# Fifth term of the first product for two of eight hidden units: from four full matmuls to pairs of 64-row matmuls beside the convolution, with a new order of all steps

## The chip, the cores and the metric

The kernel runs on one core of one Trainium2 chip. The metric is the device time of one execution in microseconds (us), the median of several runs. The engines are TensorE (PE; its weight loads are listed apart, as PEld), VectorE (DVE), ScalarE (ACT), GpSimd (POOL), and SyncE (SP), which here only issues transfers.

## The reference, cut to what matters

A causal convolution of 7 taps over 4096 tokens (8 batches, 192 channels, one softmaxed kernel per head of 24 channels) feeds a two-layer network whose activation is a rational function:

```python
out = np.einsum('hk,bskhg->bshg', softmax(weight), x_unf)      # convolution
x = out.reshape(32768, 192)
h = x @ w_in                                                   # 192 -> 2048, first product
P = a[0] + a[1] * h + a[2] * h2 + a[3] * h3
Q = 1.0 + np.abs(b[0]) * np.abs(h) + np.abs(b[1]) * h2
return ((P / (Q + 1e-06)) @ w_out).astype(np.float32)          # 2048 -> 192, second product
```

## The kernel before, in words

The 32768 tokens are 64 chunks of 512. The 2048 hidden features are eight units of 256, and each unit is two halves (j = 0, 1) of 128 features. So a chunk has: one convolution (step c), eight units of the first product (g1, two pieces a and b each), eight rational functions (steps hs, p, u, v, A, B, Q, L, Y, m, e, g, each on a tile of 128 x 1024), eight units of the second product (g2, four pieces each) and two stores (O).

The first product keeps more than one pass of precision by splitting both operands: x = xh + xl and w = wh + wl, each part rounded to the fp32r format. The 192 channels are 128 (part 0) and 64 (part 1). For part 0 three products are summed: wh xh, wl xh, wh xl. For part 1 the tile xB holds xh of the 64 channels in rows 0 to 63 and xl of the same channels in rows 64 to 127, and the weights of part 1 are stored twice, in rows 0 to 63 and again in rows 64 to 127; so wh on xB gives wh xh + wh xl in one matmul, and wl on xB gives wl xh (and the negligible wl xl) in another. That is five matmuls of 128 rows x 512 columns for each half of a unit (L362 to L369), ten for a unit, eighty for a chunk. The fifth is wl on xB.

The convolution (L304 to L313) is 72 small matmuls on tiles of 64 rows x 32 columns, two row halves by four column groups of the array, each of 58 tokens; being plain fp32, each becomes two instructions of the profile, 144 for a chunk. Its result goes to two PSUM banks (o0, o1), which the second product of the chunk before has just left; ACT copies it out rounded (xh), DVE takes the rest (xl), and small SBUF-to-SBUF transfers on SP's queue (move, gaps) put the parts in their places.

The order of the steps is written out by hand in three texts: START (chunks 0 to 2 and the preparation of the weights), PLAN (one period, repeated for chunks 3 to 62), END. A step "g16a.2" is piece a of unit 6 of the first product, of the chunk two before the period's own. Each engine executes its steps in the order of the text; semaphores hold back a step whose data or buffer isn't there. In a period PE does: the convolution of chunk i, units 6 and 7 of the first product of chunk i-2, then units 0 to 5 of chunk i-1, and between these the second product of chunk i-2. The PSUM tile of a unit (hp, ps_h) has two buffers, so a unit's first matmul waits for the last reader of the unit two before it: hs, A and B on ACT, v on DVE. The tile y (ps_y, PSUM) has one buffer: Y of a unit on ACT waits for g of the unit before on DVE, and m of a unit on DVE waits for its Y.

```python
        terms = ((wh_t, 0, xhA), (wl_t, 0, xhA), (wh_t, 0, xlA), (wh_t, 1, xB), (wl_t, 1, xB))
        for n, (w, part, x) in enumerate(terms):
            nc.tensor.matmul(H[k][:, j, :], lhsT=w[:, i, part, j, :], rhs=x, start=(n == 0), stop=(n == len(terms) - 1))
```

Of the kernel before, what the change touches and what calls it, by code (L numbers as in the profile page):

```python
# [54 lines left out]


START = """
tp1.0 tp3.0 tp2.0 tp5.0 tp4.0 tp6.0 tp8.0 tp9.0 cf0.0 cf1.0 wia0.0 wis0.0 wio0.0 cf2.0 c0.0 xh0.0 wid0.0
xl0.0 xh1.0 wia1.0 xl1.0 wis1.0 wio1.0 tp0.0 wid1.0 wir0.0 wih0.0 wil0.0 g10a.0 wir1.0 wia2.0 wis2.0
wow0.0 wiw3.0 wio2.0 wid2.0 wow1.0 wod0.0 wih1.0 woa0.0 wos0.0 woo0.0 wid3.0 wir2.0 wih2.0 wia3.0 wis3.0  # L60
wor0.0 wiw4.0 g10b.0 wio3.0 wod1.0 hs0.0 B0.0 wow2.0 woa1.0 p0.0 u0.0 wip1.0 A0.0 Q0.0 wir3.0 wid4.0
wil1.0 wos1.0 woo1.0 wia4.0 g11a.0 g11b.0 hs1.0 p1.0 tp7.0 B1.0 wor1.0 wip2.0 wis4.0 wio4.0 woa2.0
wil2.0 u1.0 A1.0 Q1.0 wos2.0 woo2.0 v0.0 wih3.0 wip3.0 wiw5.0 wia5.0 wod2.0 L0.0 wow3.0 wis5.0 wor2.0
wil3.0 wiw6.0 wid5.0 Y0.0 wio5.0 woa3.0 wow4.0 g12a.0 wir4.0 g12b.0 v1.0 hs2.0 p2.0 wos3.0 m0.0 B2.0
g13a.0 g13b.0 woo3.0 u2.0 wih4.0 wip4.0 wia6.0 wod3.0 L1.0 wor3.0 wiw7.0 A2.0 e0.0 wis6.0 g0.0 hs3.0
wio6.0 woa4.0 Q2.0 wir5.0 Y1.0 v2.0 wos4.0 p3.0 wid6.0 wir6.0 wil4.0 wih5.0 wip5.0 woo4.0 wia7.0 wow5.0
wod4.0 m1.0 u3.0 g14a.0 g14b.0 wis7.0 wid7.0 e1.0 A3.0 B3.0 wio7.0 wir7.0 wih6.0 woa5.0 hs4.0 wil5.0
v3.0 wow6.0 Q3.0 wip6.0 wow7.0 wos5.0 wil6.0 wih7.0 L2.0 g1.0 B4.0 g15a.0 woo5.0 wip7.0 g15b.0 wil7.0
c0.1 Y2.0 m2.0 A4.0 hs5.0 p4.0 xh0.1 xh1.1 u4.0 v4.0 g16a.0 Q4.0 p5.0 u5.0 xl0.1 xl1.1 e2.0 B5.0 woa6.0
A5.0 wos6.0 woo6.0 woa7.0 g2.0 wos7.0 g16b.0 woo7.0 L3.0 c0.2 Q5.0 hs6.0 v5.0 g17a.0 Y3.0 g17b.0 A6.0  # L70
xh0.2 xh1.2 m3.0 xl0.2 e3.0 g3.0 g20a.0 g20c.0 B6.0 hs7.0 p6.0 u6.0 v6.0 g21a.0 g21c.0 g22a.0 L4.0
g10a.1 g10b.1 xl1.2 g20b.0 Q6.0 p7.0 g20d.0 Y4.0 g21b.0 u7.0 m4.0 B7.0 g21d.0 g22b.0 wor4.0 A7.0 Q7.0
L5.0 L6.0 e4.0 hs0.1 g4.0 Y5.0 wod5.0 v7.0 g11a.1 p0.1 m5.0 e5.0 u0.1 wod6.0 B0.1 A0.1 g11b.1 Q0.1 hs1.1
p1.1 A1.1 g5.0 Y6.0 v0.1 m6.0 e6.0 g22c.0 g23a.0 L7.0 u1.1 g22d.0 g23b.0 wor6.0 g6.0 g23d.0 B1.1 g12a.1
v1.1 g12b.1 A2.1 Q1.1 hs2.1 Y7.0 g23c.0 g24a.0 g24b.0 g24d.0 m7.0 e7.0 L0.1 g7.0 g24c.0 g13a.1 g13b.1
wor5.0 B2.1 p2.1 wod7.0 u2.1 hs3.1 A3.1 wor7.0 g25a.0 g25c.0 g26a.0 g25b.0 g26c.0 Y0.1 v2.1 m0.1 e0.1
g0.1 g14a.1 g14b.1 g25d.0 B3.1 L1.1 hs4.1 Y1.1 Q2.1 g26b.0 g26d.0 g27a.0 B4.1 g27b.0 g27d.0 g27c.0 p3.1
u3.1 A4.1 v3.1 g15a.1 L2.1 O0.0 O1.0 m1.1 e1.1 Q3.1 p4.1 g15b.1 u4.1 g1.1 Y2.1 v4.1 Q4.1 hs5.1
"""


END = """
c0.1 xh0.1 g16a.3 g16b.3 xh1.1 m2.3 xl0.1 xl1.1 L3.3 g20a.3 g20b.3 g20d.3 g21b.3 g21d.3 g20c.3 p5.3 e2.3
A5.3 u5.3 B5.3 Q5.3 hs6.3 g2.3 v5.3 Y3.3 g17a.3 L4.3 p6.3 g17b.3 u6.3 A6.3 g21a.3 g21c.3 B6.3 Q6.3 hs7.3
p7.3 m3.3 e3.3 g3.3 g22a.3 u7.3 Y4.3 g22c.3 v6.3 g10a.2 B7.3 g10b.2 L5.3 A7.3 Q7.3 hs0.2 p0.2 u0.2 m4.3
e4.3 g4.3 g22b.3 g22d.3 g23a.3 Y5.3 A0.2 v7.3 g11a.2 L6.3 B0.2 g11b.2 g23b.3 g23d.3 g24b.3 hs1.2 p1.2
m5.3 e5.3 g5.3 v0.2 Q0.2 g23c.3 Y6.3 A1.2 g12a.2 m6.3 g12b.2 u1.2 B1.2 Q1.2 g24d.3 e6.3 g6.3 L7.3 v1.2
g24a.3 hs2.2 p2.2 g25b.3 g25d.3 Y7.3 m7.3 g13a.2 g13b.2 g24c.3 g25a.3 g25c.3 g26a.3 e7.3 g7.3 B2.2 A2.2
u2.2 v2.2 g14a.2 L0.2 Q2.2 hs3.2 Y0.2 m0.2 p3.2 L1.2 A3.2 g14b.2 g26b.3 e0.2 g26c.3 g27a.3 g0.2 B3.2
u3.2 v3.2 Q3.2 hs4.2 Y1.2 m1.2 e1.2 g1.2 L2.2 A4.2 g27c.3 O0.3 g15a.2 g15b.2 g20a.2 p4.2 u4.2 B4.2  # L90
g26d.3 g27b.3 hs5.2 Y2.2 g27d.3 v4.2 g16a.2 g16b.2 B5.2 Q4.2 O1.3 m2.2 e2.2 p5.2 u5.2 g2.2 A5.2 Q5.2
v5.2 g20c.2 g21a.2 L3.2 g20b.2 g20d.2 hs6.2 p6.2 u6.2 Y3.2 m3.2 e3.2 g3.2 L4.2 g17a.2 g17b.2 B6.2 A6.2
Q6.2 v6.2 g21b.2 g21d.2 hs7.2 Y4.2 m4.2 g21c.2 L5.2 e4.2 g4.2 p7.2 u7.2 A7.2 B7.2 v7.2 Q7.2 g10a.1
g10b.1 hs0.1 p0.1 u0.1 Y5.2 L6.2 g22a.2 g22c.2 g23a.2 g23c.2 A0.1 g11a.1 m5.2 e5.2 g11b.1 B0.1 hs1.1
g22b.2 p1.1 g5.2 g22d.2 g23b.2 Y6.2 g23d.2 A1.1 v0.1 L7.2 g12a.1 B1.1 g12b.1 hs2.1 m6.2 e6.2 g6.2 Q0.1
Y7.2 B2.1 L0.1 g24b.2 g24d.2 g25b.2 u1.1 v1.1 Q1.1 g13a.1 g13b.1 m7.2 e7.2 p2.1 u2.1 g24a.2 A2.1 g24c.2
g7.2 v2.1 g14a.1 hs3.1 p3.1 g14b.1 Y0.1 m0.1 e0.1 B3.1 Q2.1 L1.1 g25d.2 g26b.2 g0.1 A3.1 g25a.2 u3.1
hs4.1 v3.1 g15a.1 Q3.1 Y1.1 B4.1 g15b.1 m1.1 e1.1 g1.1 L2.1 A4.1 p4.1 u4.1 v4.1 hs5.1 g25c.2 g26a.2 Y2.1
m2.1 e2.1 g2.1 Q4.1 g26c.2 g27a.2 p5.1 u5.1 A5.1 B5.1 v5.1 g27c.2 Q5.1 g26d.2 g16a.1 L3.1 Y3.1 m3.1 e3.1
g27b.2 g16b.1 g17a.1 g27d.2 hs6.1 O0.2 g20a.1 p6.1 g17b.1 A6.1 O1.2 g20b.1 g20d.1 g20c.1 g21a.1 g21b.1  # L100
L4.1 g3.1 Y4.1 m4.1 g21d.1 hs7.1 e4.1 g4.1 B6.1 B7.1 g21c.1 g22a.1 L5.1 Y5.1 g22b.1 u6.1 v6.1 g22c.1
g23a.1 g22d.1 g23b.1 Q6.1 g23d.1 g24b.1 p7.1 u7.1 m5.1 e5.1 g5.1 A7.1 L6.1 v7.1 Y6.1 Q7.1 g24d.1 g25b.1
m6.1 e6.1 g6.1 L7.1 Y7.1 m7.1 e7.1 g23c.1 g24a.1 g24c.1 g7.1 g25a.1 g25c.1 g26a.1 g26c.1 g25d.1 g26b.1
g26d.1 g27a.1 g27c.1 O0.1 g27b.1 g27d.1 O1.1
"""


# [1 line left out]
def kernel(  # L109
# [251 lines left out]

    def gemm1(k, j):  # L362
        c, i = divmod(k, UPC)
        xhA, xlA, xB = X[c, "A"], X[c, "L"], X[c, "B"]
        if j == 0:
            H[k] = ps_h.tile([P, 2, CH], F32, name="hp")
        terms = ((wh_t, 0, xhA), (wl_t, 0, xhA), (wh_t, 0, xlA), (wh_t, 1, xB), (wl_t, 1, xB))
        for n, (w, part, x) in enumerate(terms):
            nc.tensor.matmul(H[k][:, j, :], lhsT=w[:, i, part, j, :], rhs=x, start=(n == 0), stop=(n == len(terms) - 1))  # L369

# [190 lines left out]
```

## Time and profile before

| | us |
|---|---|
| median of 3 runs | 2677.01 (2675.8 to 2678.11) |
| profiled execution | 2675.36 |
| its span, first to last instruction | 2673.7 |
| PE busy (matmuls) | 2636.4 (99%) |
| DVE busy | 2583.7 (97%) |
| ACT busy | 2563.2 (96%) |
| POOL busy | 2313.4 (87%) |

The profiled execution took 1.7 us more than its span. Busy time is the union of an engine's instructions; instructions of one engine overlap (the next begins while the last results of the one before are being written), so the distance from start to start is shorter than the duration. Matmul ends are modelled: starts are what is to be read on PE. The chain of waits that ended last runs over PE for 92% of the span.

### The profile page before, as it was taken

The page shows a single profiled execution, that of the slowest core. Times are in us where ns is not written, and L with a number is a line of the kernel's source. Part 1 is how long each engine was busy: PE and PEld are TensorE (multiplying, and loading weights), DVE is VectorE, ACT ScalarE, POOL GpSimd, SP SyncE. Part 2 cuts the span into 40 slices and gives each one's busy share as a digit, 9 for nine tenths or more (in the row PEclk, how much of TensorE's full clock was granted, in tenths as well). Part 3 has the DMA queues.
Part 4 walks back from the last instruction along what each step waited for, and adds up shares of the span by engine and source line. Part 5 has one row for each costly group of instructions (what it writes and reads, how often), then busy time and mean ns, then how long its engine had stood idle before and what let it go on. Part 6 is the DMA issues. An engine that isn't in the chain of part 4 may idle for free.

```text
span 2673.7 us, 56816 instructions
## 1 busy us (share of the span) xinstructions
PE 2636.4 (99%) x22513; PEld 2392.6 (89%) x22513; DVE 2583.7 (97%) x2235; ACT 2563.2 (96%) x2863; POOL 2313.4 (87%) x1565
## 2 busy tenths in 40 slices
...
GB/s 198 118 137 127 131 139 125 134 136 125 137 130 130 137 124 131 139 126 132 137 127 137 126 132 136 124 135 135 129 131 134 131 137 123 131 138 124 130 125 93
DMA packets 138706, 352.25 MB, mean 132 GB/s; under 512 B 19416, under 2 KB 54488, under 8 KB 138440
## 3 DMA queue, kind: packets, MB, share of 16 engines
...
## 4 chain that ended last, share of the span: by engine, by line
PE 92%; DVE 2%; ACT 2%; issue 2%; POOL 1%; DMA 1%; ACTq 0%; POOLq 0%; DVEq 0%
PE o L387 47%; PE hp L369 42%; PE o L312 3%; DVE t L421 1%; DVE y L444 1%; POOL t L417 1%; ACT y L436 0%; ACT hs L410 0%; ACT B L433 0%; DVE t L448 0%; ACT A L424 0%; POOL t L413 0%; ACT B L427 0%; DMA A<-B 0%; PE y L321 0%
## 5 line engine op out<-in xcount | busy, mean ns | idle before, releaser
L387 PE MATMUL o<-wo_t,t 128*128 128x192 f32 x8192 | 1404.2, 326 | 1.3 <-DVE t L448 1.3
L387 PEld LDWEIGHTS o<-wo_t,t 128*128 128x128 f32 x8192 | 1354.2, 190 | 37.2 <-DVE t L448 1.9
L417 POOL TENSOR_TENSOR t<-t,hs 128x1024 f32<-128x1024 f32 x512 | 1264.1, 2469 | 32.2
L369 PE MATMUL hp<-xh,wh_t 128*128 128x512 f32 x2048 | 868.5, 424 | 9.3 <-DVE t L421 5.5
L413 POOL TENSOR_SCALAR t<-hs,cf 128x1024 f32<-128x1024 f32 x512 | 665.0, 1299 | 195.7 <-ACT hs L410 190.9
L369 PE MATMUL hp<-xh,wl_t 128*128 128x512 f32 x2048 | 803.1, 392 | 2.6 <-DVE wl_t L299 1.9
L440 DVE SCALAR_TENSOR_TENSOR t<-t,cf,y 128x1024 f32<-128x1024 f32 x512 | 655.7, 1281 | 34.3 <-ACT y L436 25.4
L421 DVE SCALAR_TENSOR_TENSOR t<-t,cf,hp 128x1024 f32<-128x1024 f32 x512 | 652.4, 1274 | 4.4 <-ACT y L436 2.3
L448 DVE SCALAR_TENSOR_TENSOR t<-y,t 128x1024 f32<-128x1024 f32 x512 | 626.8, 1224 | 17.4
L444 DVE SCALAR_TENSOR_TENSOR y<-A,y 128x1024 f32<-128x1024 f32 x512 | 625.6, 1222 | 0.0
L410 ACT COPY hs<-hp 128x1024 f32<-128x1024 f32 x512 | 519.5, 1015 | 61.9 <-PE hp L369 23.2
L430 POOL DMA_DIRECT2D A<-B x512 | 468.4, 915 | 102.8 <-ACT B L427 69.1
L436 ACT ACTIVATE y<-B 128x1024 f32<-128x1024 f32 x512 | 531.3, 1038 | 20.0 <-DVE t L448 18.5
L433 ACT ACTIVATE B<-A 128x1024 f32<-128x1024 f32 x512 | 545.2, 1065 | 4.0 <-DMA A<-B 3.9
L424 ACT ACTIVATE A<-hp 128x1024 f32<-128x1024 f32 x512 | 528.0, 1031 | 0.8 <-PE hp L369 0.8
L427 ACT ACTIVATE B<-hp 128x1024 f32<-128x1024 f32 x512 | 528.4, 1032 | 0.0
L369 PEld LDWEIGHTS hp<-xh,wh_t 128*128 128x128 f32 x2048 | 387.1, 189 | 84.0 <-DVE t L421 6.7
L369 PEld LDWEIGHTS hp<-xh,wl_t 128*128 128x128 f32 x2048 | 387.1, 189 | 66.0 <-DVE wl_t L299 2.4
L369 PE MATMUL hp<-xl,wh_t 128*128 128x512 f32 x1024 | 401.7, 392 | 0.0
L369 PEld LDWEIGHTS hp<-xl,wh_t 128*128 128x128 f32 x1024 | 193.2, 189 | 42.6 <-issue 0.4
L312 PEld LDWEIGHTS o<-wb_t,xs 64*32 64x32 f32 x9072 | 92.7, 105 | 29.3 <-issue 27.1
L312 PE MATMUL o<-wb_t,xs 64*32 64x58 f32 (+1 forms) x9072 | 102.0, 221 | 6.9 <-issue 3.9
...
## 6 DMA issues: line engine op xcount, KB each, us to landing
A<-B POOLq DMA_DIRECT2D x512, 512.0 KB, 4.8
...
out<-ob SPq DMA_DIRECT2D x128, 192.0 KB
...
xh<-xl SPq DMA_DIRECT2D x126, 48.0 KB
...
```

Of the source, the lines that this page charges most:

```text
L369: nc.tensor.matmul(H[k][:, j, :], lhsT=w[:, i, part, j, :], rhs=x, start=(n == 0), stop=(n == len(terms) - 1))
L387: nc.tensor.matmul(op[:, t, 0:D], lhsT=g[:, j * CH + tok:j * CH + tok + P], rhs=wo_t[:, f, :], start=(f == 0 and t == 0), stop=(f == FT - ...
L413: nc.gpsimd.tensor_scalar(tile_of(k, "t", tpool), st[k]["hs"], a3, a2, ALU.mult, ALU.add)
L417: nc.gpsimd.tensor_tensor(out=t, in0=t, in1=st[k]["hs"], op=ALU.mult)
L421: nc.vector.scalar_tensor_tensor(out=t, in0=t, scalar=a1, in1=flat(k), op0=ALU.add, op1=ALU.mult)
L424: nc.scalar.activation(out=tile_of(k, "A", work), in_=flat(k), func=AF.Abs, scale=scales[0])
L427: nc.scalar.activation(out=tile_of(k, "B", work), in_=flat(k), func=AF.Square, scale=scales[1])
L433: nc.scalar.activation(out=st[k]["B"], in_=st[k]["A"], func=AF.Ln, bias=C_Q)
L436: nc.scalar.activation(out=tile_of(k, "y", ps_y), in_=st[k]["B"], func=AF.Exp, scale=-1.0)
L440: nc.vector.scalar_tensor_tensor(out=t, in0=t, scalar=a0, in1=st[k]["y"], op0=ALU.add, op1=ALU.mult)
L444: nc.vector.scalar_tensor_tensor(out=y, in0=st[k]["A"], scalar=C_Q, in1=y, op0=ALU.add, op1=ALU.mult)
L448: nc.vector.scalar_tensor_tensor(out=t, in0=st[k]["y"], scalar=2.0, in1=t, op0=ALU.subtract, op1=ALU.mult)
```

## The change

For units 5 and 6 the fifth term leaves the row of five. A step h does it for both halves of the unit: half 0 as a matmul of rows 0 to 63 (weights wl rows 0 to 63, xB rows 0 to 63), half 1 as a matmul of rows 64 to 127, with the weights' second copy and a new tile xu that holds a copy of xB's rows 0 to 63 in its rows 64 to 127. The two use different halves of the array and different PSUM banks. The negligible product wl xl is left out for these units. Which matmul starts and which ends an accumulation is counted (terms_done), since h6 stands ahead of g16a and g16b and h5 behind g15b. In the repeated period PE's order becomes g15a, g15b, h5 (end of a period), c0, h6, g16a, g16b (start of the next). The copy to xu is one more transfer of 64 rows x 2 KB for each chunk on SP's queue, behind those of xl1, into a pool of two buffers. The orders of all engines are written anew.

```diff
+HALF_UNITS = (5, 6)
 PLAN = """
-c0.0 xh0.0 xh1.0 g16a.2 g16b.2 m2.2 L3.2 xl0.0 xl1.0 B5.2 A5.2 g20b.2 e2.2 g2.2 p5.2 u5.2 g20a.2 hs6.2
-Y3.2 g20c.2 g21a.2 g21c.2 v5.2 Q5.2 p6.2 A6.2 u6.2 g20d.2 m3.2 g17a.2 g17b.2 e3.2 g22a.2 L4.2 g3.2 B6.2
...
-g25d.2 g0.1 g26b.2 g26d.2 hs4.1 g27b.2 g27d.2 Y1.1 L2.1 p4.1 O0.2 A4.1 O1.2 u4.1 v3.1 m1.1 e1.1 g1.1
-B4.1 g15a.1 g15b.1 Y2.1 v4.1 hs5.1 Q4.1
+c0.0 Y2.2 hs5.2 m2.2 A5.2 xh0.0 xh1.0 e2.2 B5.2 Q4.2 xl0.0 h6.2 xl1.0 g2.2 g16a.2 g16b.2 L3.2 hs6.2 p5.2
+u5.2 g20a.2 g20c.2 v5.2 Y3.2 g20b.2 m3.2 g20d.2 Q5.2 L4.2 g21a.2 e3.2 g17a.2 g17b.2 A6.2 p6.2 g21c.2
...
+g14b.1 hs4.1 Q3.1 g0.1 Y1.1 L2.1 g25b.2 g25d.2 g26b.2 g26d.2 g27c.2 v3.1 m1.1 B4.1 g27b.2 A4.1 g27d.2
+g15a.1 g15b.1 e1.1 p4.1 O0.2 h5.1 O1.2 u4.1 g1.1 v4.1
 """
 START = """
...
+u3.0 wil6.0 B3.0 wih7.0 wip7.0 A3.0 Q3.0 v3.0 g15a.0 L2.0 hs4.0 p4.0 woo5.0 wow7.0 wil7.0 Y2.0 m2.0
+A4.0 e2.0 c0.1 B4.0 xh0.1 xh1.1 xl0.1 g15b.0 h5.0 hs5.0 xl1.1 u4.0 v4.0 woa6.0 wos6.0 wor4.0 woo6.0 h6.0
+g16a.0 g2.0 g16b.0 L3.0 B5.0 woa7.0 wos7.0 woo7.0 A5.0 p5.0 u5.0 v5.0 c0.2 g17a.0 Q4.0 Q5.0 hs6.0 p6.0
...
+    zpool = ctx.enter_context(tc.tile_pool(name="zpool", bufs=2))
...
             gaps(xB[BLK:], xl, 104, 2)
+            upper_copy(c)
+
+    def upper_copy(c):
+        X[c, "U"] = zpool.tile([P, CH], F32R, name="xu")
+        move(X[c, "U"][BLK:], X[c, "B"][0:BLK])
...
+    terms_done = {}
+
+    def term(k, j, w, x, **kw):
+        if k not in H:
+            H[k] = ps_h.tile([P, 2, CH], F32, name="hp")
+        n = terms_done[k, j] = terms_done.get((k, j), 0) + 1
+        nc.tensor.matmul(H[k][:, j, :], lhsT=w, rhs=x, start=(n == 1), stop=(n == 5), **kw)
 
     def gemm1(k, j):
...
+        for w, part, x in ((wh_t, 0, xhA), (wl_t, 0, xhA), (wh_t, 0, xlA), (wh_t, 1, xB)):
+            term(k, j, w[:, i, part, j, :], x)
+        if i not in HALF_UNITS:
+            term(k, j, wl_t[:, i, 1, j, :], xB)
+
+    def gemm1_halves(k):
+        c, i = divmod(k, UPC)
+        for j, x in enumerate((X[c, "B"], X[c, "U"])):
+            rows = slice(BLK * j, BLK * j + BLK)
+            term(k, j, wl_t[rows, i, 1, j, :], x[rows], tile_position=(BLK * j, 0))
```

## Rows read from the trace of the kernel before

**Rows 1.** The page: busy time, share of the span and instructions of each engine.

```profile
PE 2636.4 (99%) x22513; PEld 2392.6 (89%) x22513; DVE 2583.7 (97%) x2235; ACT 2563.2 (96%) x2863; POOL 2313.4 (87%) x1565
```

**Rows 2.** Windows: stretch, length, busy of PE to POOL, granted clock, DMA.

```profile
0.00:106.30 106.30, 79.86 (x685) 63.58 (x685) 83.58 (x108) 85.17 (x116) 77.80 (x68) 0.89 0.67 164
...
1004.98:1045.77 40.79, 40.79 (x353) 37.20 (x353) 40.04 (x35) 39.63 (x45) 35.83 (x25) 1.00 0.64 132
...
2560.30:2673.70 113.40, 106.16 (x583) 95.94 (x570) 103.03 (x87) 97.61 (x107) 85.14 (x57) 1.00 0.53 106
...
147.08:2560.30 2413.22, 2409.60 (x20913) 2195.89 (x20912) 2357.61 (x2008) 2341.20 (x2598) 2115.30 (x1417) 1.00 0.64 131
```

**Rows 3.** Waits from 147.08 to 2560.30: waiter, releaser, us in total, times, longest.

```profile
PEld o L312 <- issue: 21.1, 58, 0.8
...
DVE t L440 <- ACT y L436: 16.8, 68, 0.6
...
PE hp L369 <- DVE t L421: 1.8, 3, 0.8
```

**Rows 4.** Timeline of PE around one convolution: start, us, instruction.

```profile
1004.67 0.39 PE L369 MATMUL hp<-xh,wl_t 128*128 128x512 f32 x1
1004.98 1.59 PE L312 MATMUL o<-wb_t,xs 64*32 64x58 f32 x144
1006.51 0.50 PE L369 MATMUL hp<-xh,wh_t 128*128 128x512 f32 x1
1006.84 0.39 PE L369 MATMUL hp<-xh,wl_t 128*128 128x512 f32 x1
1007.07 0.39 PE L369 MATMUL hp<-xl,wh_t 128*128 128x512 f32 x1
...
1008.92 4.06 PE L387 MATMUL o<-wo_t,t 128*128 128x192 f32 x24
```

**Rows 5.** Timeline of PE's weight loads around the same convolution.

```profile
1004.44 0.19 PEld L369 LDWEIGHTS hp<-xh,wl_t 128*128 128x128 f32 x1
1004.98 1.46 PEld L312 LDWEIGHTS o<-wb_t,xs 64*32 64x32 f32 x144 [0.35 <-issue]
1006.50 0.19 PEld L369 LDWEIGHTS hp<-xh,wh_t 128*128 128x128 f32 x1
1006.61 0.19 PEld L369 LDWEIGHTS hp<-xh,wl_t 128*128 128x128 f32 x1
```

**Rows 6.** Groups by shape: the convolution's matmuls, busy us, mean ns, idle before.

```profile
L312 PE MATMUL o<-wb_t,xs 64*32 64x58 f32 x8064 | 91.7, 221 | 3.0 <-DVE wo_t L284 3.0
```

**Rows 7.** Timeline of DVE from 1041 to 1053, over one start of a period.

```profile
1041.73 1.28 DVE L440 SCALAR_TENSOR_TENSOR t<-t,cf,y 128x1024 f32<-128x1024 f32 x1
...
1045.36 1.28 DVE L421 SCALAR_TENSOR_TENSOR t<-t,cf,hp 128x1024 f32<-128x1024 f32 x1
1046.57 1.28 DVE L440 SCALAR_TENSOR_TENSOR t<-t,cf,y 128x1024 f32<-128x1024 f32 x1
1048.00 1.29 DVE L339 TENSOR_TENSOR xl<-o,xh 128x512 fp32r<-128x512 f32 x2 [0.15 <-ACT xh L330]
...
1053.11 1.28 DVE L440 SCALAR_TENSOR_TENSOR t<-t,cf,y 128x1024 f32<-128x1024 f32 x1 [0.24 <-ACT y L436]
```

**Rows 8.** Timeline of ACT over the same start of a period.

```profile
1045.51 1.03 ACT L436 ACTIVATE y<-B 128x1024 f32<-128x1024 f32 x1 [0.24 <-DVE t L448]
1046.47 1.01 ACT L410 COPY hs<-hp 128x1024 f32<-128x1024 f32 x1
...
1052.01 1.07 ACT L436 ACTIVATE y<-B 128x1024 f32<-128x1024 f32 x1
```

**Rows 9.** Timeline of PE in START, around the convolution of chunk 2.

```profile
61.73 1.82 PE L312 MATMUL o<-wb_t,xs 64*32 64x58 f32 x128 [2.99 <-DVE wo_t L284]
66.00 0.41 PE L312 MATMUL o<-wb_t,xs 64*32 64x48 f32 x14 [2.46 <-issue]
```

**Rows 10.** The page: transfers by issuing queue: count, KB each.

```profile
xh<-xl SPq DMA_DIRECT2D x126, 48.0 KB
```

More of the change, by code (lines that the diff above doesn't have):

```diff
@@ L44 @@
 PLAN = """
-c0.0 xh0.0 xh1.0 g16a.2 g16b.2 m2.2 L3.2 xl0.0 xl1.0 B5.2 A5.2 g20b.2 e2.2 g2.2 p5.2 u5.2 g20a.2 hs6.2
-Y3.2 g20c.2 g21a.2 g21c.2 v5.2 Q5.2 p6.2 A6.2 u6.2 g20d.2 m3.2 g17a.2 g17b.2 e3.2 g22a.2 L4.2 g3.2 B6.2
-hs7.2 v6.2 g21b.2 Y4.2 g21d.2 g22b.2 L5.2 m4.2 Q6.2 e4.2 B7.2 A7.2 g10a.1 g10b.1 g4.2 p7.2 g22d.2 g23b.2
-g23d.2 g24b.2 hs0.1 u7.2 p0.1 Y5.2 A0.1 v7.2 L6.2 B0.1 m5.2 e5.2 Q7.2 g11a.1 g11b.1 hs1.1 g22c.2 g5.2
-u0.1 g23a.2 g23c.2 g24a.2 Y6.2 p1.1 Q0.1 v0.1 g12a.1 g12b.1 g24d.2 B1.1 A1.1 L7.2 m6.2 e6.2 g6.2 hs2.1
@@ L50 @@
-g25b.2 u1.1 Q1.1 p2.1 Y7.2 v1.1 B2.1 m7.2 u2.1 e7.2 g24c.2 g25a.2 A2.1 g13a.1 g13b.1 L0.1 g7.2 hs3.1
-Q2.1 Y0.1 p3.1 g25c.2 g26a.2 v2.1 g26c.2 g27a.2 m0.1 L1.1 A3.1 g14a.1 g14b.1 B3.1 u3.1 Q3.1 e0.1 g27c.2
-g25d.2 g0.1 g26b.2 g26d.2 hs4.1 g27b.2 g27d.2 Y1.1 L2.1 p4.1 O0.2 A4.1 O1.2 u4.1 v3.1 m1.1 e1.1 g1.1
-B4.1 g15a.1 g15b.1 Y2.1 v4.1 hs5.1 Q4.1
+c0.0 Y2.2 hs5.2 m2.2 A5.2 xh0.0 xh1.0 e2.2 B5.2 Q4.2 xl0.0 h6.2 xl1.0 g2.2 g16a.2 g16b.2 L3.2 hs6.2 p5.2
+u5.2 g20a.2 g20c.2 v5.2 Y3.2 g20b.2 m3.2 g20d.2 Q5.2 L4.2 g21a.2 e3.2 g17a.2 g17b.2 A6.2 p6.2 g21c.2
@@ new lines @@
+B6.2 hs7.2 u6.2 g3.2 v6.2 Y4.2 A7.2 m4.2 g21b.2 g21d.2 g22a.2 g10a.1 L5.2 Q6.2 B7.2 g10b.1 e4.2 g4.2
+p7.2 hs0.1 Y5.2 g22b.2 u7.2 p0.1 g22d.2 g23b.2 Q7.2 B0.1 A0.1 v7.2 m5.2 u0.1 e5.2 L6.2 Q0.1 g23d.2 g5.2
+g11a.1 g11b.1 g22c.2 g23a.2 g23c.2 hs1.1 Y6.2 p1.1 v0.1 A1.1 g24b.2 m6.2 e6.2 g12a.1 B1.1 g12b.1 u1.1
+Q1.1 L7.2 g24a.2 hs2.1 g24c.2 g25a.2 p2.1 g6.2 Y7.2 v1.1 m7.2 e7.2 g24d.2 g13a.1 u2.1 A2.1 g13b.1 L0.1
+g25c.2 g7.2 B2.1 v2.1 hs3.1 g26a.2 g26c.2 g27a.2 Q2.1 Y0.1 p3.1 B3.1 m0.1 e0.1 L1.1 A3.1 u3.1 g14a.1
@@ L54 @@
+g14b.1 hs4.1 Q3.1 g0.1 Y1.1 L2.1 g25b.2 g25d.2 g26b.2 g26d.2 g27c.2 v3.1 m1.1 B4.1 g27b.2 A4.1 g27d.2
+g15a.1 g15b.1 e1.1 p4.1 O0.2 h5.1 O1.2 u4.1 g1.1 v4.1
 """
 START = """
[L58 to L76, printed above, removed]
@@ L77 @@
-g0.1 g14a.1 g14b.1 g25d.0 B3.1 L1.1 hs4.1 Y1.1 Q2.1 g26b.0 g26d.0 g27a.0 B4.1 g27b.0 g27d.0 g27c.0 p3.1
-u3.1 A4.1 v3.1 g15a.1 L2.1 O0.0 O1.0 m1.1 e1.1 Q3.1 p4.1 g15b.1 u4.1 g1.1 Y2.1 v4.1 Q4.1 hs5.1
+tp8.0 tp0.0 tp1.0 tp2.0 tp3.0 tp4.0 tp5.0 tp6.0 c0.0 tp9.0 cf0.0 cf1.0 wia0.0 wis0.0 wio0.0 wid0.0
+wir0.0 xh0.0 xh1.0 xl0.0 xl1.0 wia1.0 wis1.0 wid1.0 wio1.0 cf2.0 wih0.0 wil0.0 g10a.0 wia2.0 wis2.0
+wid2.0 wio2.0 wir1.0 wih1.0 tp7.0 wow0.0 woa0.0 wos0.0 g10b.0 wiw3.0 woo0.0 wow1.0 wod0.0 wid3.0 wia3.0
@@ new lines @@
+wir2.0 wih2.0 wor0.0 A0.0 B0.0 wiw4.0 wis3.0 wio3.0 wip1.0 wil1.0 wip2.0 g11a.0 wir3.0 g11b.0 woa1.0
+wos1.0 hs0.0 woo1.0 wih3.0 wia4.0 wis4.0 wio4.0 Q0.0 wow2.0 wod1.0 wid4.0 wod2.0 woa2.0 p0.0 u0.0 wil2.0
+wip3.0 hs1.0 wos2.0 v0.0 g12a.0 wiw5.0 woo2.0 wil3.0 wor1.0 L0.0 Y0.0 m0.0 wir4.0 wia5.0 wis5.0 A1.0
+wio5.0 wow3.0 g12b.0 B1.0 B2.0 e0.0 woa3.0 wos3.0 wid5.0 wiw6.0 wow4.0 wor2.0 p1.0 wih4.0 wip4.0 woo3.0
+wia6.0 u1.0 v1.0 Q1.0 hs2.0 wis6.0 wod3.0 wiw7.0 A2.0 wir5.0 wio6.0 woa4.0 g13a.0 g13b.0 p2.0 wid6.0
@@ new lines @@
+wow5.0 u2.0 wor3.0 wih5.0 wir6.0 g0.0 wos4.0 L1.0 wil4.0 woo4.0 wia7.0 Q2.0 v2.0 wip5.0 g14a.0 g14b.0
+Y1.0 wis7.0 hs3.0 p3.0 wod4.0 wid7.0 wow6.0 wil5.0 wih6.0 wio7.0 woa5.0 wir7.0 m1.0 wip6.0 e1.0 wos5.0
+g1.0 u3.0 wil6.0 B3.0 wih7.0 wip7.0 A3.0 Q3.0 v3.0 g15a.0 L2.0 hs4.0 p4.0 woo5.0 wow7.0 wil7.0 Y2.0 m2.0
+A4.0 e2.0 c0.1 B4.0 xh0.1 xh1.1 xl0.1 g15b.0 h5.0 hs5.0 xl1.1 u4.0 v4.0 woa6.0 wos6.0 wor4.0 woo6.0 h6.0
+g16a.0 g2.0 g16b.0 L3.0 B5.0 woa7.0 wos7.0 woo7.0 A5.0 p5.0 u5.0 v5.0 c0.2 g17a.0 Q4.0 Q5.0 hs6.0 p6.0
@@ new lines @@
+Y3.0 m3.0 u6.0 wod5.0 xh0.2 xl0.2 g17b.0 g20a.0 g20c.0 xh1.2 g21a.0 g21c.0 e3.0 g22a.0 g3.0 xl1.2 B6.0
+A6.0 Q6.0 g20b.0 v6.0 g10a.1 hs7.0 p7.0 u7.0 L4.0 Y4.0 g10b.1 A7.0 B7.0 g22c.0 Q7.0 wod6.0 wor6.0 L5.0
+g23a.0 wor5.0 m4.0 e4.0 g4.0 v7.0 hs0.1 p0.1 u0.1 Y5.0 m5.0 e5.0 g23c.0 g20d.0 L6.0 g5.0 g21b.0 g11a.1
+g11b.1 B0.1 g24a.0 A0.1 Q0.1 g21d.0 g22b.0 g22d.0 v0.1 g12a.1 g12b.1 hs1.1 Y6.0 m6.0 g24c.0 g25a.0 e6.0
+g6.0 p1.1 g23b.0 A1.1 L7.0 u1.1 g23d.0 g24b.0 B1.1 Q1.1 v1.1 g24d.0 hs2.1 g13a.1 g13b.1 Y7.0 g25b.0 L0.1
```

54 lines of the change are left out of this document (27 added, 27 removed).

## The prediction

> **What bounds the kernel now.** I read the busy shares first: PE 99%, DVE 97%, ACT 96% [rows 1]. That alone doesn't tell which of three nearly full engines sets the time, so the windows come next. From the convolution of chunk 4 to that of chunk 63, 59 periods take 2413.22 us, 40.90 each, and PE is busy in 2409.60 of them [rows 2]; an ordinary period is 40.78 or 40.79 long and PE idles in none of it, while DVE has 0.75 us and ACT 1.16 us to spare. The waits confirm it: PE's first product waited 1.8 us for DVE in all 59 periods, while DVE waited 16.8 us for ACT's Y alone [rows 3]. So in the periods the path is PE's own sequence, and what PE saves there counts until the next engine is late. Outside lie START (106.30 us, PE busy 79.86) and the last stretch (113.40 us, DVE busy 103.03) [rows 2].
>
> Next, what one instruction costs on PE. Full matmuls of the first product (rows of 512 columns, below: a row) start 0.23 us apart (1006.84, 1007.07), each weight load beginning 0.23 ahead of its matmul [rows 4, 5]. At the convolution two more prices can be read. Going in, 0.31 us pass from the last row's start to the first small matmul, 0.08 more than a row; the first small weight load starts only then, PEld having idled 0.35 us with no semaphore to explain it [rows 4, 5]; 58 such idle times stand in the 59 periods [rows 3]. So at a change of shape loads don't run ahead. Coming out, the first full matmul starts at 1006.51 and the second 0.33 later instead of 0.23: its own load, started at 1006.50, is not hidden, and that costs 0.10 [rows 4, 5].
>
> **The change on PE, per chunk.** Removed: four rows (two units, two halves) at 0.23, 0.92 us. Added: two pairs of 64 rows x 512 columns, and changes of shape. No pair of this shape stands in the trace. That two row halves do work at once is shown by the convolution: 144 instructions in the 1.53 us from 1004.98 to 1006.51 are 10.6 ns each [rows 4], and even with all four column groups at once, one row half after the other would need more: 24 plain fp32 instructions of 192 columns take 4.06 us [rows 4], 0.88 ns per column, so one of 58 columns needs some 51 ns (an estimate), a quarter of which is 12.8. The margin is thin, but I take a pair as one row's time, 0.23.
>
> The changes of shape were 128x128 to 64x32 and back. They become 128x128, 64x128 (h5), 64x32 (convolution), 64x128 (h6), 128x128: four instead of two. Priced by the convolution's rows, h5 costs 0.08 (wait for an empty array) + 0.10 (load in the open) + 0.23 = 0.41; its way into the convolution is the one that stands there today. h6 takes over the convolution's way out and its open load, adds 0.23, and pays 0.08 + 0.10 to return to full rows: 0.41. Sum 0.82, gain 0.10 us per chunk.
>
> The Trainium skill, TensorEngine Tiling (Array Packing), Key Properties, says that a change of the tiling mode, unlike one of the tile alone, drains the engine. This trace agrees for 128x128 to 64x32 (0.08 and the idle load queue); whether 64x128 next to 64x32 counts as such a change no run here shows. By that rule all four changes drain and the change earns little, as in the forecast; were the shapes of 64 rows one mode, the first rival would come out.
>
> Bounds of this term: at best no new change costs anything and the loads hide, 2 x 0.23, gain 0.46 per chunk; below one row's time a pair of 512 columns can't go, as its columns stream one after another. At worst a pair is no pair: 0.92 plus two more changes at 0.18, loss 0.36. Between: the second half's load follows the first in the open, 0.10 more for each h, loss 0.10. I take +0.10, the value nearest to the one row of a switch that there is.
>
> **What is late next.** DVE. From one m to the next it takes 4.84 us when nothing is waited for (1041.73 to 1046.57), but 6.54 at the start of a period (1046.57 to 1053.11), where it waits 0.15 for ACT's xh and 0.24 for Y [rows 7]. ACT runs without a hole from Y to Y there, 1045.51 to 1052.01 [rows 8]: hs, two xh, L, B, A, hs. The new order has the same set between Y2 and Y3 (hs5, A5, two xh, B5, L3, hs6), and DVE has the same set between m2 and m3, so this stretch stays. Hence 7 x 4.84 + 6.54 = 40.42 us is the least a period can take in either order: a saving on PE over 0.36 is lost to DVE.
>
> **The other steps.** h6 is now what waits for the buffer of unit 4, so for v4, as g16a did. v4 starts at 1045.36 and ends 1.28 later, at 1046.64 [rows 7]; conv of that period starts at 1045.77 (the window's end) and lasts 1.53, so 0.65 us of slack cover it, and h5 ahead of the convolution makes it more. hs5, A5 and B5 now wait for h5, 0.41 later than g15b, but stand behind Y2, which waits for DVE's g1 anyway. The copy to xu is 128 KB per chunk beside moves like the 48 KB row [rows 10]; on SP's queue it waits for the gaps into xB and only the next chunk's load and the stores stand behind it, most of a period away; the 16 transfer engines are busy 0.64 of the time [rows 2]. Its first reader h5 comes over a period later. Cost 0, and if that cover failed, h5 and everything of PE behind it would wait as long as the copy is late.
>
> START: PE idles 26.4 of 106.3 us [rows 2]; 2.99 and 2.46 of them are the waits around chunk 2's convolution [rows 9]. The new order puts h5 and h6 of chunk 0 on PE ahead of it, and its other steps trade places with no row to price them. I take -1 us; ends: -6 (both waits go), +5 (as much again). The last stretch is DVE's: PE's small saving hardly shows, -0.5 (from -1 to +1).
>
> **The sum.** From the convolution of chunk 3 (106.30) to that of chunk 63 (2560.30) there are 60 periods. 60 x -0.10 = -6; START -1, end -0.5: -7.5 us. The profiled execution took 2675.4 (span 2673.7 and 1.7 around it), so 2667.9; it lay 1.6 under the median of 2677.0. On the median: **2669.5 us**. Its own range is 2663 to 2676, START's ends and a few hundredths per period.
>
> **Rivals.**
> 1. Shapes of 64 rows follow each other without emptying the array, and only the ends cost what they cost today. For it: inside the convolution 144 loads go through beside the matmuls in 1.46 us [rows 5], with no emptying between tiles. Against: from h5 to the convolution the columns are regrouped as well. PE would save about 0.4; DVE and ACT stop it at 0.36: 60 x -0.36 - 1.5 = -23, **2654 us**.
> 2. Slower: the two halves' loads run one after the other in the open, and so the pair's second matmul trails by 0.10. It decides as soon as an h takes over 0.46. For it: full loads start 0.11 apart at the earliest (1006.50, 1006.61 [rows 5]). Against: 144 small loads overlap in 1.46 us [rows 5]. 60 x +0.10 - 1.5: **2681.5 us**.
> 3. The change doesn't do what it says: the halves run one after the other. Against it the 10.6 ns above and the mean of 221 ns of one small matmul, of which many are in flight at once [rows 6]. 60 x +0.36 - 1.5 = +20: **2697 us**.
> 4. PE saves what I say, but a wait of the new order (h6 for v4, or Y2 for g1, with ACT's chain behind it) gives it back: **2677 us**, give or take 5.
>
> **Chances.** Forecast 0.42, rival 1 0.28, rival 2 0.15, rival 3 0.07, rival 4 0.08. A difference under 0.2% (5.4 us) can't be told from none. Faster: rival 1 and some 0.7 of the forecast's cases, with a little of rival 4, 0.58. Same: the rest of the forecast, half of rival 2, most of rival 4, 0.25. Slower: 0.17. The range leaves out rival 3 and the outer parts of rivals 1 and 2: 2652 to 2685.
>
> **What would show it.** Right: periods of 40.68 us; the first h5 matmul 0.31 after the last row of g15b, its mate within 0.02, the convolution some 0.4 behind; the first full row after h6 0.3 behind it and the next 0.33 after that; PE without waits. Rival 1: periods of 40.4, PE waiting for DVE at g2 or g1. Rival 2: mates 0.1 apart in their ends, periods of 40.9. Rival 3: 0.23 between mates. The prediction is wrong if PE has idle time in every period, or START moves by over 6 us.

## The result: 2697.7 us, slower by 0.75%

The changed kernel takes 2697.74 us (median of 6 runs, 2693.98 to 2701.39) against 2677.53 for the kernel before: ratio 1.0075, 95% interval 1.0062 to 1.0088. Forecast were 2669.5, range 2652 to 2685. The time is that of rival 3 (2697), but by chance and from another cause: the pairs do run as pairs.

The profiled execution has a span of 2699.7 us, 26.0 more than before. It is the slowest of the six, where the medians are 20.2 us apart, so what is counted in it below is somewhat more than the 20 us of the medians. The page, busy time by engine [rows 1] and two of the transfer queues:

```profile
PE 2645.9 (98%) x22513; PEld 2373.3 (88%) x22513; DVE 2580.0 (96%) x2235; ACT 2565.3 (95%) x2863; POOL 2308.4 (86%) x1565
...
q1 hardware_dynamic: 69544, 88.51, 11.5%
q8 instruction: 177, 2.90, 0.4%
```

Where in time it went is read from the windows, which answer to [rows 2] (stretch, length, busy of PE to POOL, granted clock, DMA). The last two lie inside the period of the line ahead of them.

```profile
0.00:105.48 105.48, 80.08 (x686) 61.80 (x686) 83.57 (x109) 85.33 (x116) 77.92 (x68) 0.90 0.68 171
...
146.34:2584.72 2438.38, 2417.14 (x20770) 2178.46 (x20768) 2353.24 (x2007) 2342.28 (x2597) 2109.65 (x1416) 1.00 0.65 133
...
1055.49:1096.30 40.81, 40.81 (x354) 36.82 (x352) 39.91 (x35) 39.66 (x45) 35.77 (x24) 1.00 0.66 135
...
804.40:849.80 45.40, 42.53 (x355) 38.11 (x354) 39.87 (x35) 39.79 (x45) 35.67 (x24) 0.96 0.59 121
806.00:810.00 4.00, 1.13 (x5) 0.62 (x6) 3.93 (x5) 3.35 (x5) 3.92 (x3) 1.00 0.82 219
810.00:814.00 4.00, 4.00 (x13) 3.45 (x13) 0.67 (x1) 1.22 (x2) 0.27 (x2) 0.58 0.79 155
```

START is 0.8 us shorter (106.30 before). Forecast was -1, but a difference of this size shows nothing: three kernels with the START of before, it and two of the experiments below, have 106.30, 105.44 and 106.54 us. The ordinary period is 40.82, 0.04 longer than before. But 59 periods take 2438.38 us, 41.33 each: 30 us more than 59 x 40.82. Before it was 6 us more than 59 x 40.78: the convolution of chunk 63 starts there at 2558.90, not at the 2560.30 of the prediction, which is near that convolution's end, so that 59 periods are 2411.82 us. Single periods are 1 to 5 us longer now, and in them PE stands idle although DVE, ACT and POOL work on. In the waits of that stretch (waiter, releaser, us in total, times, longest) PE's and PEld's large entries have no engine as releaser, only "issue"; in [rows 3] the longest of these was 0.8 us:

```profile
PEld hp L375 <- issue: 43.2, 121, 3.4
...
PEld o L314 <- issue: 18.0, 62, 1.8
...
PEld o L407 <- issue: 9.8, 6, 2.5
PE o L407 <- issue: 9.0, 6, 2.3
PE hp L375 <- issue: 7.1, 3, 3.2
...
PE o L314 <- issue: 4.1, 4, 1.6
```

Of PEld's 43.2 us, the bulk of the 121 times is the two new changes of shape in each period; entries of 1.5 to 3.4 us are something else. One of these holes on PE's timeline, just behind a convolution that starts at 804.39:

```profile
805.92 0.50 PE L375 MATMUL hp<-xh,wl_t 64*128 64x512 f32 x1
805.92 0.50 PE L375 MATMUL hp<-xu,wl_t 64*128 64x512 f32 x1
806.35 0.50 PE L375 MATMUL hp<-xh,wh_t 128*128 128x512 f32 x1
806.69 0.40 PE L375 MATMUL hp<-xh,wl_t 128*128 128x512 f32 x1
809.97 0.59 PE L375 MATMUL hp<-xl,wh_t 128*128 128x512 f32 x1 [2.87 <-issue]
```

It falls in the middle of a unit, between two matmuls with the same buffer and the same kind of operands, where no semaphore is waited for. What such holes have in common comes out by counting. Worked out from the trace's records, for each distance over 0.6 us between starts on PE: PE's loads, matmuls and semaphore instructions up to there, in blocks of 256, and the last 16 KB packet on queue q8, the "instruction" queue, that started before PE went on. (q8 carries 177 packets. PE has 45026 loads and matmuls and 400 semaphore and drain instructions, 45426 in all, which is 177.4 blocks of 256, so a packet is one block of PE's instructions.)

```
changed kernel (9 of 15)                     packet of q8
hole from   distance us  blocks of 256     start     landed    PE goes on
 272.71       2.44          17.75          272.89    273.85    275.15
 435.77       1.06          28.75          434.58    435.46    436.83
 644.31       1.75          42.75          643.72    644.68    646.05
 806.69       3.28          53.75          807.72    808.60    809.97
1343.08       1.85          89.75         1342.75   1343.71   1344.93
1553.75       2.09         103.75         1553.46   1554.39   1555.83
2086.77       3.58         139.75         2088.17   2089.11   2090.34
2462.22       2.64         164.75         2462.53   2463.41   2464.86
2274.62       1.13         151.66   (hp's release by DVE, no fetch)
```

Thirteen of the 15 lie 63 or 64 instructions short of a multiple of 256 with PE going on 1.2 to 1.5 us after a packet has landed; the other two (0.67 us at 1181.63, 1.13 us at 2274.62) are waits for DVE. (The first of these stands at such a count too, but the profile names DVE as its releaser, and with the count shifted, below, it comes at the same place of the period.) So in the thirteen PE's sequencer, which hands PE its instructions and is by this some 64 of them ahead of the array, has come to the end of what has been fetched. The convolution uses 288 instructions in 1.53 us, more than a packet; elsewhere a packet lasts some 24 us.

A packet starts, in the median, 0.4 us (kernel before) or 0.8 us (changed) after the sequencer has come to the end of a block, and what it carries is needed at the end of the next block. If a block ends early in a convolution, the next one ends 1.3 to 5.6 us after the convolution's start, at the places of the holes. The count gives, for each packet, when it was asked for in this sense. In the kernel before, of 32 packets asked for in the first 0.65 us of a convolution 31 start at most 2.6 us after its start; those asked for later in it mostly start 3.5 to 5.1 us after it, and no hole follows them. In the changed kernel 23 of the 32, and all 36 of the later ones, start 3.3 to 4.5 us after it. What is in their way is on POOL's timeline, the issue of the 512 KB accumulation of unit 4 (Q4). Kernel before, its convolution at 1045.77:

```profile
1045.56 0.88 POOL L430 DMA_DIRECT2D A<-B  x1 [1.02 <-ACT B L427]
```

Changed kernel, its convolution at 1055.49:

```profile
1053.87 0.89 POOL L450 DMA_DIRECT2D A<-B  x1 [0.26 <-ACT A L444]
1056.82 1.20 POOL L433 TENSOR_SCALAR t<-hs,cf 128x1024 f32<-128x1024 f32 x1 [2.06 <-ACT hs L430]
```

Issued 0.2 us ahead of the convolution before, 1.6 us ahead now (the new order ends ACT's period with B4, A4, O0, O1 instead of A4, O1, B4). In the mean of 57 periods the accumulation's own packets fill the 16 transfer engines from 0.2 to 3.1 us after the convolution's start, where before they did so from 1.3 to 4.2: an instruction packet asked for early in the convolution went ahead of them before, and comes behind them now.

The sum: the 15 holes are 26.0 us in all, 23 without the ordinary distance of some 0.2 each. Four of them are followed by 3.4 us at the lower clock level, as in the window from 810.00 to 814.00 (mean 0.58; the levels are 1.2 and 2.4 GHz) behind a stretch in which PE was busy 1.13 of 4.00 us; at half speed each loses some 1.7, together 7. That is about the 30 us. Before, 6 holes of 4.7 us (three of them, 2.6 us, are waits for DVE) gave 3.5 of the 6; what the rest is was not traced. So 24 us come from holes and clock, and 60 x 0.04 = 2.4 from the ordinary periods, together the 26.6 by which the 60 periods from chunk 3's convolution to chunk 63's grew (2452.6 to 2479.2).

### The profile page after: what moved, and what is told of

It is laid out like the page before. It is cut to its first block, busy times and chain, and to the rows that moved or that the text cites. A ratio compares the mean times of both kernels' runs of the same rounds, so it can differ in the third digit from the quotient of the medians.

```text
span 2699.7 us, 56896 instructions
## 1 busy us (share of the span) xinstructions
PE 2645.9 (98%) x22513; PEld 2373.3 (88%) x22513; DVE 2580.0 (96%) x2235; ACT 2565.3 (95%) x2863; POOL 2308.4 (86%) x1565
## 4 chain that ended last, share of the span: by engine, by line
PE 84%; issue 4%; DVE 4%; POOL 3%; ACT 2%; DMA 1%; SPq 1%; ACTq 0%; POOLq 0%; DVEq 0%
PE o L407 43%; PE hp L375 38%; PE o L314 3%; POOL t L437 2%; DVE t L441 2%; DVE y L464 2%; POOL t L433 1%; DVE t L468 1%; SPq L360 1%; ACT hs L430 1%; ACT y L456 1%; ACT B L447 0%; DMA raw<-in_w_in 0%; ACT A L444 0%; ACT xh L332 0%
## 5 line engine op out<-in xcount | busy, mean ns | idle before, releaser
L437 POOL TENSOR_TENSOR t<-t,hs 128x1024 f32<-128x1024 f32 x512 | 1246.7, 2435 | 37.6
L433 POOL TENSOR_SCALAR t<-hs,cf 128x1024 f32<-128x1024 f32 x512 | 648.5, 1267 | 254.4 <-ACT hs L430 241.0
L375 PE MATMUL hp<-xh,wh_t 128*128 128x512 f32 x2048 | 851.2, 426 | 8.8 <-DVE t L441 4.8
L375 PE MATMUL hp<-xh,wl_t 128*128 128x512 f32 (+1 forms) x1920 | 767.8, 400 | 6.1 <-issue 3.2
L375 PEld LDWEIGHTS hp<-xh,wl_t 128*128 128x128 f32 (+1 forms) x1920 | 362.5, 189 | 87.0 <-issue 26.3
```

What stands on the lines that cost most here:

```text
L375: nc.tensor.matmul(H[k][:, j, :], lhsT=w, rhs=x, start=(n == 1), stop=(n == 5), **kw)
L433: nc.gpsimd.tensor_scalar(tile_of(k, "t", tpool), st[k]["hs"], a3, a2, ALU.mult, ALU.add)
L437: nc.gpsimd.tensor_tensor(out=t, in0=t, in1=st[k]["hs"], op=ALU.mult)
```

## The experiments

Times of the runs: medians, with the ratio to the kernel before on the same chip (2677.53 us for the changed kernel, 2678.18 for the next four, 2679.15 for the last four). Holes: distances over 0.6 us on PE between the convolutions of chunks 3 and 63, number and sum, counted as above; of fetch: those 63 or 64 instructions short of a block's end and not waits for DVE.

| kernel | us | ratio (95%) | holes, us | of fetch | ordinary period |
|---|---|---|---|---|---|
| before | 2677.53 | 1 | 6, 4.7 | 3, 2.1 | 40.78 |
| changed | 2697.74 | 1.0075 (1.0062 to 1.0088) | 15, 26.0 | 13, 24.2 | 40.82 |
| new order, late Q4 | 2679.51 | 1.0001 (0.9992 to 1.0010) | 8, 9.1 | 6, 7.4 | 40.82 |
| new order, five rows | 2696.49 | 1.0066 (1.0052 to 1.0079) | 13, 22.3 | 12, 21.1 | 40.85 |
| old order, pairs | 2676.13 | 0.9989 (0.9980 to 0.9998) | 8, 8.3 | 5, 5.8 | 40.75 |
| old order, early Q4 | 2688.56 | 1.0037 (1.0023 to 1.0051) | 12, 18.4 | 9, 15.5 | 40.78 |
| old order, pairs, late Q4 | 2677.53 | 0.9992 (0.9983 to 1.0001) | 8, 9.5 | 6, 7.6 | 40.75 |
| old order, late Q4 | 2679.76 | 1.0003 (0.9994 to 1.0012) | 8, 8.1 | 5, 5.2 | 40.80 |
| new order, shifted | 2705.05 | one run | 18, 29.4 | 16, 27.6 | 40.82 |
| old order, double pair | 2696.01 | one run | 10, 10.4 | 8, 8.1 | 40.96 |

**The new order with Q4 later.**

```diff
-c0.0 Y2.2 hs5.2 m2.2 A5.2 xh0.0 xh1.0 e2.2 B5.2 Q4.2 xl0.0 h6.2
+c0.0 Y2.2 hs5.2 m2.2 A5.2 xh0.0 xh1.0 e2.2 B5.2 z4.2 Q4.2 xl0.0 h6.2
+    def step_z(k):
+        for _ in range(3):
+            nc.gpsimd.memset(idle_t, 0.0)
```

> The changed kernel with one thing more: three memsets of an unused tile on POOL ahead of Q4 in the period, in time in which POOL waits anyway, so that the 512 KB accumulation of unit 4 is issued about 1.9 us later, near the start of the convolution instead of 1.6 us before it. Theory (instruction fetch): the extra time of the changed kernel is holes on PE at every 256th instruction pair, because the 16 KB packet with PE's next instructions waits behind this transfer until 4 us after the start of the convolution. Then the packets start 1 to 2 us after it, the 15 holes (26 us in the profiled execution) shrink to under 8 us, and the time falls from 2697.7 to 2675 to 2683. Rival A (the pairs and their copy cost the time): unchanged, 2694 to 2701. Rival B (the new order starves PE through DVE or ACT): unchanged or slower.

(The count is of 256 instructions, loads and matmuls together, not of pairs.) Measured 2679.51 us, 1.3 over the kernel before on its chip, where the changed kernel is 20.2 over: 19 of the 20 us are gone, with pairs, copy and order left as they were. POOL's timeline there, its convolution at 678.65:

```profile
676.71 2.01 POOL L455 MEMSET idle_t<- 128x640 f32 x3
678.67 0.89 POOL L451 DMA_DIRECT2D A<-B  x1
```

Q4 is issued at the convolution's start and its packets fill the transfer engines from 1.6 to 4.7 us after it; all 32 packets asked for in a convolution's first 0.65 us now start at most 1.8 us after its start, and no stretch of the lower clock is left in the periods. Rivals A and B fall as causes of the 20 us. (Holes came to 9.1 us, not under 8; two of the eight are waits for DVE.)

**The new order without pairs.** HALF_UNITS is empty, step h does nothing, the copy to xu is not made.

```diff
-HALF_UNITS = (5, 6)
+HALF_UNITS = ()
...
             elif kind == "h":
-                gemm1_halves(c * UPC + n)
+                pass
```

> The new order with the fifth term as full rows in all units again: step h does nothing, no copy to xu. Theory (instruction fetch): Q4 still goes ahead of the convolution, so the holes stay at the 256-instruction boundaries; 2690 to 2699. Rival A (pairs or copy): back to the time before, 2674 to 2680. Rival B (the order): slower than before as well, but with PE waiting on DVE or ACT by semaphores rather than in holes that nothing releases.

Measured 2696.49: 18.3 of the 20.2 us without any pair. Its 12 fetch holes stand at 12 of the 13 counts of the changed kernel, the first again at 17.75 blocks:

```profile
275.33 3.25 PE L405 MATMUL o<-wo_t,t 128*128 128x192 f32 x19 [1.97 <-issue]
```

**The old order with pairs.** The texts of before, with h5 behind each g15b and h6 ahead of each g16a:

```diff
-B4.1 g15a.1 g15b.1 Y2.1 v4.1 hs5.1 Q4.1
+B4.1 g15a.1 g15b.1 h5.1 Y2.1 v4.1 hs5.1 Q4.1
```

> The old order with h5 put behind g15b and h6 ahead of g16a, and the copy to xu; nothing else moved. Theory (instruction fetch): Q4 is issued 0.2 us before the convolution as before, so holes stay near the 5 us of before; the pairs themselves come out about even (two of them at 0.43 for four rows at 0.227, and some rows a few ns slower, +0.04 us in an ordinary period): 2676 to 2683. Rival A (pairs or copy): 2692 to 2702.

Measured 2676.13, at the lower end: the pairs gain 0.03 us in an ordinary period where I expected a loss of 0.04. That loss belongs to the new order: with five rows its ordinary period is 40.85, 0.07 more than the old order's, its PE rows standing about 1 ns further apart on average (244.0 against 243.1). Why is open. The holes did not stay near 5 us: 8.3, and of fetch 5.8 against 2.1, though Q4 is issued at the same place; this, too, is open. It takes what the ordinary periods gain, so that the 60 periods come to 2453.1 us against 2452.6 before.

**The old order with Q4 earlier**, and no pair:

```diff
-... Y1.1 L2.1 p4.1 O0.2 A4.1 O1.2 u4.1 v3.1 m1.1 e1.1 g1.1
-B4.1 g15a.1 g15b.1 Y2.1 v4.1 hs5.1 Q4.1
+... Y1.1 p4.1 A4.1 O0.2 B4.1 O1.2 L2.1 u4.1 v3.1 m1.1 e1.1 g1.1
+g15a.1 g15b.1 Y2.1 v4.1 hs5.1 Q4.1
```

> The kernel before, without any pair, with ACT's order at the end of the period changed to A4, O0, B4, O1, L2 so that Q4 can be issued some 1.0 us earlier, about 1.2 us before the convolution. Theory (instruction fetch): holes as in the changed kernel appear without any of its pairs: 2687 to 2700. Rival A and B: no pair and nearly the old order, 2674 to 2681.

Measured 2688.56. Q4 issues 1.3 us ahead of the convolution (678.54, convolution at 679.83), and the kernel before now has 12 holes of 18.4 us, nine of fetch where it had three, one of 3.11 us of idle time at the same 53.75 blocks as in the changed kernel, with 3.4 us of the lower clock behind it. So the place of this one transfer makes a loss of 10 us in the old order and takes away that of 20 in the new.

```profile
678.54 0.87 POOL L430 DMA_DIRECT2D A<-B  x1
```

```profile
808.45 0.59 PE L369 MATMUL hp<-xh,wl_t 128*128 128x512 f32 x1 [3.11 <-issue]
```

**The new order, shifted.** 32 more small matmuls (128 instructions, half a packet) ahead of the first convolution.

```diff
     def conv_start(cps):
+        for _ in range(32):
+            nc.tensor.matmul(cps[0][0:32, 0:BW], lhsT=x0_buf[0][:, 0:32], rhs=wb_t[:, START_GROUPS[0], 0:BW], start=True,
+                             stop=True, tile_position=(0, 0))
```

> The changed kernel with 32 more small matmuls ahead of the first convolution, 128 more PE instructions once in START, half a fetch packet; they write what the first small matmul writes. Theory (instruction fetch): all holes stay 64 instructions short of a multiple of 256 in PE's own count, so they come in other periods than in the changed kernel (not near 272.7, 644.3, 806.7 us), about as many and about as long: 2690 to 2706. Rival A (a resource that collides by time, without PE's instruction count): holes in the same periods as in the changed kernel.

Measured 2705.05, one run (START is 5.4 us longer than in the changed kernel; why is open). All holes but the two that are waits for DVE (0.68 and 1.13 us) again lie 64 short of a block's end, at 12.75, 23.75, 34.75, 37.75, 48.75 blocks and so on, but at 197.5, 360.2, 523.3, 569.6, 731.6 us; none near 272.7, 644.3 or 806.7. They follow PE's instruction count, not the period; the two waits for DVE stay at their places of the period.

**Q4 later in the old order**, with pairs and without: the same step z (three memsets) ahead of Q4.1 in PLAN.

> The old order with the pairs, and three memsets of an unused tile (2.0 us) on POOL ahead of Q4 in the period, so that Q4 is issued some 0.8 us after the start of the convolution instead of 0.2 us before it. Theory (instruction fetch): the packets that PE needs during the convolution find the transfer engines free of the accumulation; the 8.3 us of holes in the profiled execution of the old order with pairs shrink to 2 to 6 us; 2670 to 2676. Rival (what holes are left has nothing to do with Q4): 2675 to 2678.

> The kernel before with the same three memsets ahead of Q4 and no other edit. Theory (instruction fetch): its 4.7 us of holes shrink by 1 to 4 us: 2673 to 2677. Rival (holes have nothing to do with Q4): 2676 to 2680.

Measured 2677.53 and 2679.76: my expectation missed in both, no fetch hole went away (holes 9.5 and 8.1 us, against 8.3 and 4.7 without the delay; of fetch 7.6 and 5.2 against 5.8 and 2.1, so that there are rather more of them; why is open). Of the 4.7 us not all was fetch to begin with: three of those six holes are waits for DVE. Most of the fetch holes that are left come at 28.75, 64.75, 89.75 and the like: there a packet starts between 0.4 us ahead of a convolution and 0.7 after its start, and what it carries is needed 1.3 to 1.5 us after that start, within the convolution itself; the 0.9 us or more that a packet takes and the 1.2 to 1.6 to PE's restart are already more than that. They are the convolution's own, and 0.2 us of lead for Q4 was small enough. The lowest time remains that of the old order with pairs, 0.11% under the kernel before, clear of 1 by its interval alone; that the pairs gain this is not shown, since in the profiled executions START alone accounts for it (104.64 against 106.30 us, and 105.90 in the same START with the delay).

**A second pair without a change of shape.** The pair of unit 5 is issued twice in a row, so that its term is added twice.

```diff
         for j, x in enumerate((X[c, "B"], X[c, "U"])):
             rows = slice(BLK * j, BLK * j + BLK)
+            if i == 5:
+                nc.tensor.matmul(H[k][:, j, :], lhsT=wl_t[rows, i, 1, j, :], rhs=x[rows], start=False, stop=False,
+                                 tile_position=(BLK * j, 0))
+        for j, x in enumerate((X[c, "B"], X[c, "U"])):
+            rows = slice(BLK * j, BLK * j + BLK)
             term(...)
```

> The old order with pairs, with the pair of unit 5 issued twice in a row (its term is then added twice): the price of a pair without a change of shape ahead of it. If the change of shape is what makes a pair cost 0.43 us, the second pair costs 0.22 to 0.25, or 0.33 with its load in the open, and the ordinary period goes from 40.75 to 40.97 to 41.09; if 64-row pairs are slow by themselves, the second costs 0.43 as well: 41.18.

```profile
1055.55 0.39 PE L375 MATMUL hp<-xh,wh_t 128*128 128x512 f32 x1
1055.87 0.49 PE L390 MATMUL hp<-xh,wl_t 64*128 64x512 f32 x1
1055.87 0.50 PE L390 MATMUL hp<-xu,wl_t 64*128 64x512 f32 x1
1056.20 0.39 PE L375 MATMUL hp<-xh,wl_t 64*128 64x512 f32 x1
1056.21 0.38 PE L375 MATMUL hp<-xu,wl_t 64*128 64x512 f32 x1
1056.52 1.60 PE L314 MATMUL o<-wb_t,xs 64*32 64x58 f32 x144
```

From the first pair to the convolution 0.65 us, where a single pair has 0.43: the second costs 0.22, one row's time, and the ordinary period 40.96 says the same (0.21). So 0.2 of a pair's 0.43 us is the change of shape. The time, 2696.01, is one run; 60 x 0.21 is 13 us of it, and START is 6.4 us longer than with single pairs, which is open too.

## Why the prediction was wrong, step by step

**The pairs: right.** The changed kernel's PE timeline around an ordinary convolution, to be held against [rows 4]:

```profile
1054.75 0.39 PE L375 MATMUL hp<-xh,wh_t 128*128 128x512 f32 x1
1055.07 0.49 PE L375 MATMUL hp<-xh,wl_t 64*128 64x512 f32 x1
1055.07 0.49 PE L375 MATMUL hp<-xu,wl_t 64*128 64x512 f32 x1
1055.49 1.60 PE L314 MATMUL o<-wb_t,xs 64*32 64x58 f32 x144
1057.02 0.50 PE L375 MATMUL hp<-xh,wl_t 64*128 64x512 f32 x1
1057.02 0.50 PE L375 MATMUL hp<-xu,wl_t 64*128 64x512 f32 x1
1057.45 0.50 PE L375 MATMUL hp<-xh,wh_t 128*128 128x512 f32 x1
1057.79 0.40 PE L375 MATMUL hp<-xh,wl_t 128*128 128x512 f32 x1
```

h5 starts 0.32 after the last row, both mates within 0.01, the convolution 0.42 behind; the full rows go on 0.43 behind h6, the second 0.34 after. Forecast were 0.31, 0.02, 0.4, 0.3 and 0.33. The 0.3 is a slip of the list of signs: the sum has 0.41 there. At all four changes of shape the first load starts only with its first matmul:

```profile
1055.07 0.18 PEld L375 LDWEIGHTS hp<-xh,wl_t 64*128 64x128 f32 x1 [0.36 <-issue]
...
1055.49 1.46 PEld L314 LDWEIGHTS o<-wb_t,xs 64*32 64x32 f32 x144 [0.24 <-issue]
1057.02 0.18 PEld L375 LDWEIGHTS hp<-xh,wl_t 64*128 64x128 f32 x1
...
1057.45 0.19 PEld L375 LDWEIGHTS hp<-xh,wh_t 128*128 128x128 f32 x1 [0.25 <-issue]
```

So the array is emptied at each, as the Trainium skill's rule in TensorEngine Tiling (Array Packing), Key Properties, has it. The second pair shows the other side of the rule: within one shape nothing is emptied, its loads start at 1055.97, 0.23 ahead of its matmuls, and it costs 0.22. Rivals 1, 2 and 3 are out.

**The size of that term: too large.** I put a pair at 0.41 and a row at 0.23; measured are 0.43 and 0.227. 4 x 0.227 - 2 x 0.43 is 0.05 per chunk, not 0.10, and 0.03 is what the old order's ordinary period shows (40.78 to 40.75). Over 60 periods 2 to 3 us instead of 6: next to nothing. With the new order the ordinary period is longer than before even so (40.82).

**What is late next, START and the end: not tested.** DVE's 40.42 was never reached. START moved by -0.8 us, within what it differs by from run to run; the last stretch, from the convolution of chunk 63, by +0.2.

**The failed step is "The other steps", which the sum has at cost 0.** I priced the moved steps by what waits for them over semaphores: h6 for v4, hs5 for h5, the copy on SP's queue. I looked at the transfer engines only through their mean share, 0.64, and never compared when Q4 is issued in the two orders; it goes 1.4 us further ahead of the convolution, and behind it waits a transfer that no line of the kernel issues, PE's own next instructions. The price of that is some 20 us, against a gain of 2. The sign was readable ahead. In the 59 periods PE is idle for 3.62 us [rows 2], of which the waits for DVE are 1.8 [rows 3]; the rest has "issue" as the only reason, inside the convolution and inside a unit (waits of the kernel before from 147.08 to 2558.9):

```profile
PEld o L312 <- issue: 20.7, 57, 0.8
...
PE o L312 <- issue: 1.5, 3, 0.7
...
PE hp L369 <- issue: 0.4, 2, 0.2
```

Three holes over 0.6 us stand there at 63 or 64 short of a block's end (53.75, 64.75 and 89.75 blocks, 2.1 us in all). I put all 58 idle times of [rows 3] down to the change of shape, which costs PEld 0.35 us, although the longest there is 0.8: that one, at 965.52, is such a hole in the middle of a convolution. Nor would my sign for being wrong, idle time on PE in every period, have caught it: the fetch holes come in 13 of the 60 periods.

Rival 4 had the form (what PE saves is given back by the new order) but named semaphore waits, and at the most 5 us.
